# Key-value products in five sets of positions, and the first batch's loads and order of a float32 attention and expert kernel

## The chip, the cores and the metric

The kernel runs on one core of a Trainium2 chip. The metric is the time of one execution on the device in microseconds (us), as a median over runs. An engine of the core (TensorE or PE, VectorE or DVE, ScalarE or ACT, GpSimd or POOL, SyncE or SP) executes its own instructions in order; engines and transfers wait for each other through semaphores. "PEld" in a profile is TensorE's loading of stationary operands.

## The reference

All arrays are float32. Eight batches of eight heads with 576 positions of 64 numbers go through a linear attention with normalised rows, and the result, as 4608 tokens of 512, through four experts whose outputs are summed with normalised probabilities.

```python
kv = np.einsum('bhsd,bhse->bhde', k, v)          # q, k, v: (8, 8, 576, 64)
out = np.einsum('bhsd,bhde->bhse', q, kv)
rms = np.sqrt(np.mean(out * out, axis=-1, keepdims=True) + 1e-06)
x = (out / rms * g_norm)                          # to (4608, 512)
p = domain_probs / (domain_probs.sum(-1, keepdims=True) + 1e-09)
for e in range(4):                                # w1: (4, 512, 1024), w2: (4, 1024, 512)
    h = np.maximum(x @ w1[e], 0.0)
    out += p[:, e:e + 1] * (h @ w2[e])
```

## The kernel before

**Tiles and stages.** The tokens are nine chunks of 512: chunk b holds the first 512 positions of batch b, and the ninth holds the last 64 positions of all eight batches. A stage s is one expert with one chunk, 36 stages in all; TensorE's row of stages is the long part of the kernel. Attention of batch 0 stands at the very start, that of batch c + 1 is woven into stage c of the first expert. The matrix products of the experts use schemes with seven products in place of eight, at two levels (`up`, line 914 in the profile, for x by w1; `down`, line 1128, and `down_deep`, line 1203, for h by w2), so that sums of blocks of weights, of x and of h must be formed beforehand: `combine` (line 362) on DVE or POOL. The first stage's x by w1 is a plain product, `up_plain` (line 1001).

**Attention of a batch** works on four pairs of heads. A pair's q (128 partitions by four positions by two heads), k and v are loaded by SP (`load`, line 368). q is turned by four transpositions on TensorE (line 653) and copied by ACT (line 658). The key-value product (line 667, `key_values`) puts 96 partitions of k and v side by side, each with six positions (KP = 96, KR = 6): for each of the six it adds one product per head, 64 columns by 64, into one bank, the two heads in different halves of its partitions. ACT copies the sums (line 680); `attend` (line 693) multiplies q by them; `scaled` squares (ACT, line 566), sums (DVE, line 573), takes the power -1/2 (POOL, lines 580 and 584) and multiplies (DVE, line 593); the result is turned again (line 711) and copied with the gain by ACT (line 719). Batch 0 handles one pair at a time, the others two (`groups`). The last 64 positions of a batch go the same way in one piece: lines 737, 755, 771.

**Hardware passes.** A float32 product is executed as two passes and a transposition as one; the profile counts passes.

**Order.** No engine's order is written by hand. Each operation is added to a `Plan` with a key (its place in the stages) and a cost that the author gives; `layout` runs a small model of the engines and takes the operations in the order of keys and due times. It also gives out the buffers: `kv` has four slots, `big` 29, `small` eight, and the banks of PSUM are pairs `u1`, `u2`, `db`, `ab`. SP's loads are taken in strict order of keys, and at most eight transfers are in flight (`LANES`); the ninth waits for the landing of the first. Where the plan sees TensorE without data ahead of the first stage, it lays fillers (`idle`, line 1355): two transpositions of the identity into a free bank.

Keys that matter here: `attention(0, -2.0, 1.3, 0.1)`, `weights_1(0, -2.5, 0.02, 0.3)` (loads of the first expert's w1 and the place of its sums), `x_forms(0, 0.3)` (sums of x), `weights_2(0, 0.25, 0.02, 7.6)`, and in `up_plain`

```python
op = plan.add(
    key + span * i / 8 - (1.1 if i < 2 and dh == 0 else 0.0), pe(2, NT), product,
```

Of the kernel before, what the change touches and what calls it, by code (L numbers as in the profile page):

```python
# [232 lines left out]
def kernel(  # L233
# [36 lines left out]
    nc = tc.nc  # L270
# [4 lines left out]
    NT = 512  # L275
# [3 lines left out]
    NCH = B + 1  # L279
    HN = NT // 2  # L280
    HF = F // 2
    KR = 6
    KP = S // KR
    EPS = 1e-6
    NBLK = NCH * NR
    assert H * D == DM == NT and D == 64 and P == 128 and NPAIR == 4 and F == 1024
    assert REM == D and REM * B == NT and KP * KR == S and KP <= P

    const = ctx.enter_context(tc.tile_pool(name="const", bufs=1))
    pool = ctx.enter_context(tc.tile_pool(name="pool", bufs=1))  # L290
# [75 lines left out]
    def load(key, buf, dst, src, kb, reads=(), also=()):  # L366
        plan.add(
            key, SPC, lambda eng: nc.sync.dma_start(out=dst(), in_=src), reads=reads,  # L368
            parts=[buf] + list(also), kb=kb,
        )  # L370
# [232 lines left out]
    def attention(b, key, span, rem):  # L603
# [6 lines left out]
        at = lambda j: key + span * j / (NPAIR + 1)  # L610
        qTs, kvs = {}, {}

        def load_pair(hp):
            hs = slice(2 * hp, 2 * hp + 2)
            n = f"{b}_{hp}"
            kind = "kv" if b or hp < 2 else "big"
            kt, vt, qt = Buf(kind, f"k{n}"), Buf(kind, f"v{n}"), Buf("small", f"q{n}")
            want = at(hp) - 0.25 if b else key - 1 + 0.1 * hp
            for r in range(2):
                load(  # L620
                    want, qt,
                    lambda qt=qt, r=r: qt.ap[:].rearrange(
                        "p (r h d) -> p r h d", h=2, d=D)[:, :, r, :],
                    q[b, 2 * hp + r, 0:NT, :].rearrange("(p r) d -> p r d", r=NR), 128 if b else 157,
                )
            for t, src in ((kt, k), (vt, v)):
                load(
                    want, t,
                    lambda t=t: t.ap[0:KP, 0:2 * KR * D].rearrange("p (h x) -> p h x", h=2),
                    src[b, hs].rearrange("h (p j) d -> p h (j d)", j=KR), 288 if b else 241,  # L630
                )
            return kt, vt, qt

        def kv_rows(t):
            return t.ap[0:KP, 0:2 * KR * D].rearrange("p (h j d) -> p h j d", h=2, d=D)

        groups = ((0,), (1,), (2,), (3,)) if b == 0 else ((0, 1), (2, 3))
        for g, pairs in enumerate(groups):
# [4 lines left out]
            for o, hp in enumerate(pairs):  # L643
                kvs[hp] = kv, o
                kt, vt, qt = load_pair(hp)
                held.append((kt, vt))
                bank = Buf("ab", f"qT{b}_{hp}")
                qT = qTs[hp] = Buf("small", f"qT{b}_{hp}")

                def turn(eng, bank=bank, qt=qt):  # L650
                    for r in range(NR):
                        rs = slice(r * P, (r + 1) * P)
                        nc.tensor.transpose(bank.ap[:, rs], qt.ap[:, rs], ident[:])  # L653

                plan.add(at(hp), pe(4, P, 1), turn, reads=[qt], writes=[bank])
                plan.add(
                    at(hp), act(NT),
                    lambda eng, bank=bank, qT=qT: nc.scalar.activation(
                        out=qT.ap[:], in_=bank.ap[:], func=ACT.Copy),
                    reads=[bank], writes=[qT],  # L660
                )

            def key_values(eng, bank=kbank, held=held):
                for o, (kt, vt) in enumerate(held):
                    for j in range(KR):
                        for r in range(2):
                            nc.tensor.matmul(  # L667
                                bank.ap[r * D:(r + 1) * D, o * D:(o + 1) * D],
                                lhsT=kv_rows(kt)[:, r, j, :], rhs=kv_rows(vt)[:, r, j, :],
                                start=(j == 0), stop=(j == KR - 1), skip_group_check=True,  # L670
                            )

            size = len(pairs)
            plan.add(
                at(pairs[-1]), {"PE": 0.73 * size + 0.2}, key_values,
                reads=[t for ts in held for t in ts], writes=[kbank],
            )
            plan.add(
# [2 lines left out]
                    out=to.ap[:, 0:size * D], in_=bank.ap[:, 0:size * D], func=ACT.Copy),  # L681
                reads=[kbank], writes=[kv],
            )
            raw = [Buf(("db", "u2")[r] if b == 0 else "ab" if b > 1 else "db", f"raw{n}_{r}") for r in range(2)]

            def attend(eng, raw=raw, kv=kv, pairs=pairs):
                for o, hp in enumerate(pairs):
# [300 lines left out]
    def up_plain(s, e, c, key, span):  # L988
# [4 lines left out]
        for i in range(8):  # L993
            uh, a, u = i // 4, i // 2 % 2, i % 2
            bank = Buf("u1" if a == 0 else "u2", f"up{s}_{i}")
            for dh in range(2):
                w, low = corners[uh, dh]

                def product(eng, w=w, bank=bank, dh=dh, ut=2 * a + u):
# [5 lines left out]
                        )  # L1005

                op = plan.add(
                    key + span * i / 8 - (1.1 if i < 2 and dh == 0 else 0.0), pe(2, NT), product,
                    reads=[w, low, xh[dh]], **({"parts": [bank]} if dh else {"writes": [bank]}),
                )  # L1010
                op.marks = bank, NT
# [297 lines left out]

    plan.add(-2.85, {"SP": 1.1}, load_gains, writes=[gains], kb=1)  # L1310
    attention(0, -2.0, 1.3, 0.1)
    sums_1 = weights_1(0, -2.5, 0.02, 0.3)
    up_plain(0, 0, 0, 0.0, 1.0)
    sums_1()
    x_forms(0, 0.3)
    x_views = {}
    inner = {0: weights_2(0, 0.25, 0.02, 7.6)}
    norm_probs(0.3)
    for e in range(E):
        for c in range(NCH):  # L1320
            s = e * NCH + c
            if e == 0 and c + 1 < B:
                attention(c + 1, s - 0.1, 0.8, s + 0.5)
            if e + 1 < E and c == NCH - 1:
                weights_1(e + 1, s + 0.0, 0.12, s + 0.4)()
                inner[e + 1] = weights_2(e + 1, s + 1.0, 0.13, s + 1.55)
            if s + 1 < E * NCH:
                if e == 0 and c + 1 < NCH:
                    x_views[s + 1] = x_forms(c + 1, s + 0.7)
# [76 lines left out]
```

## Time and profile before

| What | Value |
|---|---|
| median of 7 runs | 1717.48 us (1717.08 to 1717.93) |
| profiled execution, its own time | 1717.84 us |
| its span, first to last instruction | 1716.0 us |
| TensorE's granted clock | 0.999 of full speed |
| TensorE's passes | 15564 |
| DVE, ACT, POOL busy | 72%, 57%, 40% of the span |
| DMA, 24 to 66 us | 95% of 16 engines, 262 GB/s |
| DMA, 420 us to the end | 50% of 16 engines, 123 GB/s |

A row of a timeline gives the start and the length in us of a run of like instructions, then engine, line, operation, the tiles written and read, the shape, and the number of passes. Lengths overlap by the latency of a pass, since passes are pipelined: what a run costs is the distance from its start to the start of the next row. A row of the waits gives the engine and line that waited, who ended the wait, the total, the count and the longest.

### The profile page before, as it was taken

The numbers are of one execution on the slowest core, as the hardware profiler recorded it, in microseconds if no ns is written. First come the engines' busy times: TensorE is split into PE (matmuls) and PEld (weight loads), VectorE is DVE, ScalarE is ACT, GpSimd is POOL, SyncE is SP. The second block draws the span as 40 slices with busy tenths as digits, with TensorE's granted clock in tenths as the row PEclk, the third lists the DMA queues.
The fourth block names the chain that finished last, engine by engine and source line by source line (L and its number), as shares of the span: only waits on it lengthen the run. The fifth ranks groups of instructions, "written<-read, shape, count | busy, mean of one in ns | idle before, by whom it ended". The sixth has DMA issues, their size and how long they took to land.

```text
span 1716.0 us, 39187 instructions
## 1 busy us (share of the span) xinstructions
PE 1709.1 (100%) x15564; PEld 1651.3 (96%) x15564; DVE 1239.2 (72%) x1992; ACT 973.5 (57%) x2378; POOL 692.4 (40%) x655
## 2 busy tenths in 40 slices
PE   9999999999999999999999999999999999999998
PEld 7799999999999999999999999999999999999998
DVE  4855565466678887777788787777788787777774
ACT  3455454455446556565666566656666666666562
POOL 3533332233433432333355554433355544433331
PEclk9999999999999999999999999999999999999999
DMA  9854543543365445353568444444478444444442
GB/s 234 277 165 145 182 145 123 149 142 142 130 160 148 107 109 113 97 116 102 140 178 178 114 106 111 111 112 112 112 182 200 111 112 111 112 111 111 102 108 49
DMA packets 156567, 230.42 MB, mean 134 GB/s; under 512 B 49888, under 2 KB 97248, under 8 KB 156384
## 3 DMA queue, kind: packets, MB, share of 16 engines
q1 hardware_dynamic: 133312, 191.21, 36.4%
q0 software_dynamic: 23072, 36.71, 14.2%
q8 instruction: 122, 2.00, 0.5%
q14 instruction: 61, 0.50, 0.1%
HBM read 154.74 MB, written 73.14 MB: 133 GB/s over the span
## 4 chain that ended last, share of the span: by engine, by line
PE 99%; DMA 1%; SPq 0%; issue 0%; DVE 0%
PE u L914 45%; PE db L1203 21%; PE ab L1203 13%; PE db L1128 12%; PE u L1001 2%; PE ab L667 1%; PE ab L711 1%; PE ab L693 1%; PE ab L653 1%; PE u L1128 1%; DMA big<-in_v_dram 0%; PE ab L1128 0%; DMA kv<-in_v_dram 0%; SPq L368 0%; PE ab L755 0%; PE ab L771 0%
## 5 line engine op out<-in xcount | busy, mean ns | idle before, releaser
L362 DVE TENSOR_TENSOR big<-big,big 128x1024 f32<-128x1024 f32 (+1 forms) x435 | 437.9, 1019 | 16.7 <-ACT big L897 6.6
L914 PE MATMUL u<-xf,big 128*128 128x128 f32 x2816 | 412.5, 275 | 0.0
L914 PE MATMUL u<-xf,w1y 128*128 128x128 f32 x2652 | 391.2, 275 | 0.0
L914 PEld LDWEIGHTS u<-xf,big 128*128 128x128 f32 x2816 | 364.3, 192 | 2.0
L941 DVE TENSOR_TENSOR big<-u,snap 128x256 f32<-128x256 f32 x436 | 183.7, 421 | 239.7 <-PE u L914 155.5
L914 PEld LDWEIGHTS u<-xf,w1y 128*128 128x128 f32 x2652 | 343.7, 192 | 1.7
L933 ACT ACTIVATE snap<-u 128x256 f32<-128x256 f32 x490 | 187.5, 383 | 185.3 <-PE u L914 152.3
L362 POOL TENSOR_TENSOR big<-big,big 128x256 f32<-128x256 f32 (+1 forms) x138 | 183.4, 1344 | 164.3 <-DVE big L362 45.0
L933 ACT ACTIVATE big<-u 128x256 f32<-128x256 f32 x436 | 166.4, 383 | 99.1 <-PE u L914 73.5
L1128 PE MATMUL db<-big,big 128*128 128x256 f32 x920 | 217.0, 380 | 0.0
L1128 PEld LDWEIGHTS db<-big,big 128*128 128x128 f32 x920 | 166.8, 190 | 18.6
L1203 PE MATMUL db<-big,big 128*128 128x128 f32 x1304 | 178.1, 275 | 0.0
L1203 PEld LDWEIGHTS db<-big,big 128*128 128x128 f32 x1304 | 161.7, 192 | 0.1
L897 ACT ACTIVATE big<-big 128x1024 f32<-128x1024 f32 x126 | 132.4, 1051 | 4.5 <-DVE big L362 3.1
L1231 ACT ACTIVATE snap<-db 128x256 f32<-128x256 f32 x216 | 76.8, 356 | 102.1 <-PE db L1203 98.6
L362 POOL TENSOR_TENSOR big<-big 128x512 f32<-128x512 f32 (+1 forms) x67 | 82.2, 1229 | 119.3 <-DVE big L362 60.0
L1098 POOL DMA_DIRECT2D out_dram<-big x100 | 90.6, 1031 | 56.2 <-ACT big L1075 37.0
L1269 POOL TENSOR_TENSOR big<-big 128x512 f32<-128x512 f32 x26 | 33.0, 1269 | 198.3 <-DVE big L362 168.5
L914 PE MATMUL u<-xf,small 128*128 128x128 f32 x720 | 108.4, 275 | 0.0
L933 ACT ACTIVATE u<-u 128x256 f32<-128x256 f32 x245 | 90.9, 371 | 29.4 <-PE u L914 13.2
L1203 PE MATMUL ab<-kv,big 128*128 128x128 f32 x740 | 106.0, 275 | 0.0
L1203 PE MATMUL db<-kv,big 128*128 128x128 f32 x720 | 103.3, 275 | 0.0
(211 smaller groups left out, 2872.8 us busy)
## 6 DMA issues: line engine op xcount, KB each, us to landing
xf<-x SPq DMA_DIRECT2D x108, 512.0 KB, 3.7
out_dram<-big POOLq DMA_DIRECT2D x84, 256.0 KB, 5.8
xf<-x_h SPq DMA_DIRECT2D x81, 256.0 KB, 3.1
xf<-x SPq DMA_DIRECT2D x81, 256.0 KB, 3.3
x<-xf SPq DMA_DIRECT2D x36, 512.0 KB, 3.7
big<-in_moe_w_dram SPq DMA_DIRECT2D x31, 512.0 KB, 5.7
small<-in_q_dram SPq DMA_DIRECT2D x72, 128.0 KB, 4.2
kv<-in_k_dram SPq DMA_DIRECT2D x30, 288.0 KB, 4.5
```

Source lines behind the costliest of these rows:

```text
L362: lambda eng: adder(eng).tensor_tensor(out=out_(), in0=a(), in1=b(), op=op),
L653: nc.tensor.transpose(bank.ap[:, rs], qt.ap[:, rs], ident[:])
L897: lambda eng: nc.scalar.activation(out=b.ap[:], in_=b.ap[:], func=ACT.Relu),
L914: nc.tensor.matmul(ps.ap[:, u * P:(u + 1) * P], lhsT=w1f[e][m][mm][1]()[:, u * P:(u + 1) * P], rhs=views[m][mm][1](), start=(mm in (1, 5) ...
L933: lambda eng: nc.scalar.activation(out=where(), in_=ps.ap[:, 0:HN], func=ACT.Copy),
L941: lambda eng: nc.vector.tensor_tensor(out=block(whole, a, t), in0=src.ap[:, 0:HN], in1=add_.ap[:], op=ALU.add),
L1001: nc.tensor.matmul(bank.ap[:], lhsT=two(w.ap[:])[:, kt, ut * P:(ut + 1) * P], rhs=two(xh[dh].ap[:])[:, kt, :], start=(dh == kt == 0), stop ...
L1098: nc.gpsimd.dma_start(out=dst, in_=cell(i)[parts, :], accum_op=ALU.add)
L1128: nc.tensor.matmul(ps.ap[:, 0:HN], lhsT=four(h[m])[:, kt // 2, t, kt % 2, :], rhs=w2f[e][m].ap[:, kt * HN:(kt + 1) * HN], start=(m in (1, ...
L1203: nc.tensor.matmul(ps.ap[:, o * P:(o + 1) * P], lhsT=b.ap[:, col:col + P], rhs=w2q[e][m][mm][1]()[:, kt, :], start=(mm in (1, 5) and o == ...
L1231: lambda eng: nc.scalar.activation(out=where(), in_=group_of(ps.ap), func=ACT.Copy),
L1269: lambda eng: adder(eng).tensor_tensor(out=whole(to), in0=whole(a), in1=whole(b), op=ALU.add),
```

## The change

- **Key-value products.** In batches 1 to 7, k and v are laid in two parts: 120 partitions with four positions each (480 positions), and 96 partitions with one (the last 96). `key_values` then has five sets in place of six, four with 120 rows and one with 96. Each of k and v is loaded in two transfers, with pieces of 1024 and 256 bytes in place of 1536. Batch 0 keeps six positions on 96 partitions. The planner's cost of the product for these batches is 0.61 per pair in place of 0.73.
- **First batch's q.** One load per pair in place of two, in pieces of 1024 bytes (four positions of one head) in place of 256. The heads now lie one after the other, and the turn is eight products with the identity, 64 columns of stationary operand each, in place of four transpositions.
- **First batch's banks.** The two raw results of a pair are in `db`, `u2`, `u1`, `db` for pairs 0 to 3, in place of one in `db` and one in `u2` for every pair.
- **`up_plain`.** The first-half products of i = 0 to 3 (not 0 and 1) get an early key, in the order 2, 3, 0, 1.
- **Keys.** Small shifts for the sums of w1, of x and of w2, for batch 1, and for later experts' weights. Through the planner they move instructions on all engines.

In the program of instructions TensorE has 56 key-value products fewer (384 to 328), 54 fillers for 92, and for batch 0 32 products in place of 16 transpositions. SP issues 56 loads of k and v more and four of q fewer. DVE has 32 instructions more, POOL 32 fewer.

```diff
+        splits = ((120, 4, 0), (96, 1, 480)) if b else ((96, 6, 0),)
...
-            for r in range(2):
+            if b == 0:
                 load(
-                    want, qt,
-                    lambda qt=qt, r=r: qt.ap[:].rearrange(
-                        "p (r h d) -> p r h d", h=2, d=D)[:, :, r, :],
-                    q[b, 2 * hp + r, 0:NT, :].rearrange("(p r) d -> p r d", r=NR), 128 if b else 157,
-                )
+                    want, qt, lambda qt=qt: qt.ap[:].rearrange("p (h x) -> p h x", h=2),
+                    q[b, hs, 0:NT, :].rearrange("h (p r) d -> p h (r d)", r=NR), 172,
+                )
...
             for t, src in ((kt, k), (vt, v)):
-                load(
-                    want, t,
-                    lambda t=t: t.ap[0:KP, 0:2 * KR * D].rearrange("p (h x) -> p h x", h=2),
-                    src[b, hs].rearrange("h (p j) d -> p h (j d)", j=KR), 288 if b else 241,
-                )
+                at_ = 0
+                for rows, n_, size in splits:
+                    kb = rows * n_ // 2
+                    load(
+                        want, t,
+                        lambda t=t, at_=at_, rows=rows, n_=n_: t.ap[0:rows, at_:at_ + 2 * n_ * D]
+                        .rearrange("p (h x) -> p h x", h=2),
+                        src[b, hs, size:size + rows * n_].rearrange("h (p j) d -> p h (j d)", j=n_),
+                        kb if b else 241,
+                    )
+                    at_ += 2 * n_ * D
...
-                        nc.tensor.transpose(bank.ap[:, rs], qt.ap[:, rs], ident[:])
+                        if b:
+                            nc.tensor.transpose(bank.ap[:, rs], qt.ap[:, rs], ident[:])
+                            continue
+                        for o in range(2):
+                            at = (o * NR + r) * D
+                            nc.tensor.matmul(
+                                bank.ap[o * D:(o + 1) * D, rs], lhsT=qt.ap[:, at:at + D],
+                                rhs=ident[:],
+                            )
...
-                    for j in range(KR):
+                    sets = list(zip(kv_rows(kt), kv_rows(vt)))
+                    for j, (ks, vs) in enumerate(sets):
                         for r in range(2):
                             nc.tensor.matmul(
                                 bank.ap[r * D:(r + 1) * D, o * D:(o + 1) * D],
-                                lhsT=kv_rows(kt)[:, r, j, :], rhs=kv_rows(vt)[:, r, j, :],
-                                start=(j == 0), stop=(j == KR - 1), skip_group_check=True,
+                                lhsT=ks[r], rhs=vs[r], start=(j == 0),
+                                stop=(j == len(sets) - 1), skip_group_check=True,
                             )
...
-            raw = [Buf(("db", "u2")[r] if b == 0 else "ab" if b > 1 else "db", f"raw{n}_{r}") for r in range(2)]
+            kind = ("db", "u2", "u1", "db")[g] if b == 0 else "ab" if b > 1 else "db"
+            raw = [Buf(kind, f"raw{n}_{r}") for r in range(2)]
...
-                    key + span * i / 8 - (1.1 if i < 2 and dh == 0 else 0.0), pe(2, NT), product,
+                    key - 0.89 + 0.01 * (i ^ 2) if i < 4 and dh == 0 else key + span * i / 8,
+                    pe(2, NT), product,
...
-    sums_1 = weights_1(0, -2.5, 0.02, 0.3)
-    up_plain(0, 0, 0, 0.0, 1.0)
+    sums_1 = weights_1(0, -2.50, 0.02, 0.26)
+    up_plain(0, 0, 0, 0.0, 1.00)
     sums_1()
-    x_forms(0, 0.3)
+    x_forms(0, 0.45)
     x_views = {}
-    inner = {0: weights_2(0, 0.25, 0.02, 7.6)}
-    norm_probs(0.3)
+    inner = {0: weights_2(0, 0.25, 0.04, 7.60)}
+    norm_probs(0.30)
...
-                attention(c + 1, s - 0.1, 0.8, s + 0.5)
+                attention(c + 1, s - 0.1 + 0.03 * (s == 0), 0.8, s + 0.5)
...
-                weights_1(e + 1, s + 0.0, 0.12, s + 0.4)()
-                inner[e + 1] = weights_2(e + 1, s + 1.0, 0.13, s + 1.55)
+                weights_1(e + 1, s + 0.0, 0.12, s + 0.47)()
+                inner[e + 1] = weights_2(e + 1, s + 1.00, 0.13, s + 1.54)
```

## The prediction

> **What bounds the kernel now.** I read the busy shares, then the chain of waits, then TensorE's waits, then the timeline of the first 66 us. The page says TensorE works all the time:
>
> ```profile
> PE 1709.1 (100%) x15564; PEld 1651.3 (96%) x15564; DVE 1239.2 (72%) x1992; ACT 973.5 (57%) x2378; POOL 692.4 (40%) x655
> PE 99%; DMA 1%; SPq 0%; issue 0%; DVE 0%
> ```
>
> The other engines have room, and the chain is TensorE except for 1%. TensorE's list of waits has two entries:
>
> ```profile
> PE ab L1355 <- POOL ident masks.py:199: 1.4, 1, 1.4
> PE ab L667 <- DMA big<-in_v_dram: 1.0, 1, 1.0
> ```
>
> So the time is the sum of TensorE's instructions plus 2.4 us. But "busy" includes fillers (L1355), products of the identity that the planner lays where it expects TensorE to lack data. The start in TensorE's timeline (start, length; x counts hardware passes, two for each float32 product, one for a transposition):
>
> ```profile
> 1.35 4.96 PE L1355 MATMUL ab<-ident 128*128 128x128 f32 x22 [1.35 <-POOL ident masks.py:199]
> 6.10 0.98 PE L653 MATMUL ab<-ident,small 128*128 128x128 f32 x4
> ...
> 18.79 0.82 PE L1355 MATMUL ab<-ident 128*128 128x128 f32 x6
> 20.58 0.92 PE L667 MATMUL ab<-big,big 96*64 96x64 f32 x24 [0.97 <-DMA big<-in_v_dram]
> ...
> 23.79 3.60 PE L1001 MATMUL u<-big,big 128*128 128x512 f32 x8
> 27.22 0.60 PE L711 MATMUL ab<-ident,big 128*128 128x128 f32 x4
> 27.66 1.26 PE L1355 MATMUL ab<-ident 128*128 128x128 f32 x10
> 28.75 0.60 PE L711 MATMUL ab<-ident,big 128*128 128x128 f32 x4
> ...
> 33.65 0.60 PE L653 MATMUL ab<-ident,small 128*128 128x128 f32 x4
> 34.18 0.68 PE L755 MATMUL db<-kvbd,small 64*64 64x64 f32 x16
> 34.79 1.62 PE L667 MATMUL ab<-kv,kv 96*64 96x64 f32 x48
> 36.34 1.98 PE L1001 MATMUL u<-big,big 128*128 128x512 f32 x4
> ```
>
> Dense work begins at 23.79; before it fillers stand in for data. The last v of the first batch lands at 20.44 (7.87 us after its issue, in the chain):
>
> ```profile
> 12.57 7.87 DMA big<-in_v_dram
> ```
>
> Outside the span of 1716.0 lie 1.84 us of the profiled execution's 1717.84; that execution is 0.36 above the median of 1717.48. I sum against 1717.84 and take off 0.36. Measurement tells about 0.2% (3.4 us) from no change.
>
> **1. Five sets for six, batches 1 to 7.** A set is two heads by two passes. The L667 group of 24 passes runs from 12.06 to the next row at 12.91 (0.85), that of 48 from 34.79 to 36.34 (1.55): 24 passes are six sets in 0.70, so a set is 0.117 us. 28 pairs drop one: **-3.28 us**. Passes follow 64 columns, and the timeline cannot show a 120-row pass. Bounds: dearer by 25% for 25% more rows would give +0.8 instead; the 64-, 96- and 128-row rows of equal width show no such growth (64-row and 96-row passes last 221 to 224 ns alike), so I take -3.28.
> One rule speaks against this edit. Going from 128*128 to a narrower form and back costs extra: L653's four passes take 0.44 before a wide product (28.75 to 29.19 for L711's like), 0.53 before a narrow one (33.65 to 34.18); the first narrow pass pair is 0.05 late, the way back 0.10: about 0.12 a change. The Trainium skill, "TensorEngine Tiling (Array Packing)", Key Properties, says that changing the tiling mode drains TensorE. The new groups mix 120 and 96 rows, three row changes in each of 14 groups. If those are mode changes they cost 42 x 0.15 = 6.3 us. The page's list of modes has only 128, 64 and 32 rows, so 96 and 120 would be one mode and cost 0. No row here has 120 rows; I take 0 and keep 6.3.
>
> **2. Loads of k and v in two parts.** 56 loads more, on SP's queue. Each part is a wait of L667, and behind it on TensorE stands everything. From the third batch on, v lands 9.7 to 29 us ahead of L667 (landing 63.34, use 73.02, is the tightest), while SP issues take 0.45 to 0.62: four more for two pairs, about 2 us, are hidden. In batch 1 the slacks are 0.94 (landing 33.85, use 34.79) and 3.55 (48.15, 51.70): counted in 5. The remainder has 256-byte pieces; "DMA: Bandwidth & Descriptors", Specifications, wants 512 bytes or more for full rate. By the packet records of this trace 256-byte pieces take 18 to 21 ns and 1536-byte ones 91 to 94, 13 and 16 bytes per ns: nearly the same. By the row a remainder of 12 pieces per engine is 0.24 us and the four-set part (16 pieces of 1024, 46 to 56 ns) 0.8 to 0.9, in all like the 1.1 of now[...].
>
> **3. The start.** q of batch 0 comes in one load of 1024-byte pieces per pair: SP issues four loads fewer (0.55 to 0.63 each) and 256 KB take 0.75 to 0.97 us instead of about 1.1. Its turn becomes eight products of 64 columns, 16 passes. No row shows them; nearest is L667, where two column halves overlap (a pair of passes in 58 ns at 64 columns), so 111 ns per pair at 128 columns: 0.89 per turn for 0.44. Bounds: 0.44, and 1.74 if halves do not overlap (+3.4 in all, partly in place of the wait for v).
> The instruction order of the new kernel gives TensorE's row to the first L1001; with fillers at 0.216 until about 6.5 us (22 in 4.75) and 0.109 after: 18 fillers to 5.24; turn (half pace) 6.9; 10 fillers 8.1; keys-values 0.75 to 8.85; turn 0.89 to 9.74; attention (32 passes) 0.68 to 10.42; 4 fillers 10.95; keys-values 11.70; turn 12.59; attention 13.27; 6 fillers 14.02; keys-values 14.77; turn 15.66; attention 16.34; 2 fillers and L711's kind 17.09; fourth keys-values 17.94; 8 fillers, L711's kind, attention, 6 fillers 20.6. That is **-3.2** if data are there.
> Are they? v of pair 3 must land by 17.1 instead of 20.44. The first load's second half alone saves about 1 to 1.5 us before bandwidth binds (q lands at 3.45 and 5.48 now), each later pair 0.12 to 0.35: landing 17.5 to 19.0. Taken 18.0: a wait of **+0.9** (bounds 0.4 and 3.4, the last if v lands as now). What comes after it in order, L711's kind and L1001, is late with it; the first w1 load lands 1.1 after v and is not later.
>
> **4. Sums and products reordered.** Up products i = 2, 3, 0, 1 start before the halves of x are complete, so the ten fillers at 27.66 go: **-1.09**. The chain of pair 3 (squares, sum, power on POOL 1.9, two products) ends 4.3 us after its attention now (23.1 to 27.4); the new order leaves 0.66 + 3.44 + 0.44 + 1.72 = 6.3 before its L711: no wait.
> From the first L1001 on the new order changes form 93 times, the old 102: 9 x 0.12 = **-1.1**. DVE and POOL exchange sums (31 more small ones on DVE); DVE is idle 28% of the span and POOL 60%, which covers it; without cover the 31 would cost 0.28 each.
>
> **5. New waits in the stretch to 66 us**, where everything is some 3 us early. The transposition of batch 1's remainder (L771 now) follows two L711 groups directly and needs a bank that ScalarE must first copy out: 0.2 + 0.69 + 0.1 after the first group against 0.44 of the second: **+0.5** (0 to 1.1). Batch 1's first keys-values come at 21.5 + 3.44 + 0.44 + 1.72 + 0.44 + 1.72 + 0.53 + 0.39 + 1.72 + 0.53 = 32.4. Its v lands at 33.85 now; 2.4 earlier, as pair 3's does, and up to four issues of 0.5 later gives 31.5 to 33.5: **+0.5** (0 to 1.5). The second L1128 needs h6: relu, POOL 2.35, DVE 1.2, now 5.9 us after the last L1001 (64.9 to 70.76, slack 0.26); new order 0.97 + 0.5 + 0.39 + 1.73 + 0.88 + 0.45 = 4.9, POOL free a little earlier: **+0.5** (0 to 1.5). Behind them on TensorE waits all that follows.
>
> Sum: -3.28 - 3.2 + 0.9 - 1.09 - 1.1 + 0.5 + 0.5 + 0.5 = -6.3. 1717.84 - 6.3 = 1711.5; median **1711.2**.
>
> **Rivals.**
> A, no new wait: without the 2.4 us, 1708.8. Against: 20.58 already waits for v. 0.12.
> B, the start is bound by v as now, q's pieces hide nothing: L667 at 20.5, then 0.85 + 0.87 + 0.53 + 0.63 + 0.66: L1001 at 24.0, +0.25 for -2.3; TensorE no longer early, other waits 1.0 for 1.5: -6.3 + 2.55 - 0.5 = -4.2, time 1713.3. For: 7.87 from issue to landing shows a deep queue. 0.20.
> C, row changes drain: 1711.2 + 6.3 = 1717.5, the change does nothing one can measure. For: each change of form in the rows costs 0.12 or so. Against: the page's modes. 0.12.
> D, slower: SP's queue. Between 17.10 and 42.18 SP issues without rest, and issues of k and v there last 0.45 to 1.80. Eight more fall before batch 1's two groups. Each costing t delays the second group by 8t, less its 3.55 slack and the 2.4 that data come earlier, plus the 3.2 that TensorE comes earlier: wait 8t - 2.75. At 1.8 that is 11.65, in place of 0.5: 1722.4. It decides from the t that eats the gain and 3.4 more: 8t - 2.75 = 0.5 + 6.3 + 3.4, t = 1.6. Against: the usual issue is 0.5, and the same bytes move. 0.06.
>
> **How the numbers follow.** The main case has 0.50: 1711.2, its own range 1709 to 1714. Its gain passes 3.4 us, as do A's and B's: faster 0.82. C is the no-change case: 0.12. D: 0.06. The range leaves out D and most of C and takes the bounds in: 1708.4 to 1716.5.
>
> **What would show it.** L667 groups of 40 passes in 1.32 us between starts, without a step at the 96-row set (C: 1.7 or more). First L1001 at 21 to 22 (B: 24). L667's wait for v near 1 us; new waits at L771's and L1128's kind below 1.5 each. After 66 us no wait. It is wrong if L667 groups keep 1.55, if waits of several us stand before 66 us, or if experts' rows wait at all.

## The result and the profile after

The changed kernel takes 1713.24 us (median of 15 runs, 1711.52 to 1715.05), the kernel before beside it 1717.24 (35 runs, 1716.47 to 1720.36): a ratio of 0.9975 (95% interval 0.9968 to 0.9982), a gain of 4.0 us for 6.3 foretold. The profiled execution has a span of 1711.3 us and a time of its own of 1713.09; that of before had 1716.0 and 1717.84.

The page of the changed kernel: busy shares, the queue that brings instructions (packets, MB, share of the DMA engines), and the chain of waits.

```profile
PE 1701.6 (99%) x15462; PEld 1644.0 (96%) x15462; DVE 1229.6 (72%) x2024; ACT 971.6 (57%) x2378; POOL 693.9 (41%) x623
...
q8 instruction: 122, 2.00, 0.5%
...
PE 97%; POOL 1%; DVE 1%; DMA 1%; issue 0%; ACT 0%; POOLq 0%; DVEq 0%; ACTq 0%
```

TensorE is busy 7.5 us less and the span is only 4.7 us shorter: waits have come. TensorE's list of waits has six entries now, for two before:

```profile
PE ab L697 <- issue: 1.7, 1, 1.7
PE ab L1387 <- POOL ident masks.py:199: 1.4, 1, 1.4
PE u L945 <- ACT snap L964: 0.9, 1, 0.9
PE db L1160 <- DVE big L591: 0.5, 1, 0.5
PE ab L802 <- ACT big L750: 0.5, 1, 0.5
PE ab L1387 <- issue: 0.4, 1, 0.4
```

Lines have moved: L697 is the key-value product (L667 before), L678 the first batch's turn of q, L724 the attention, L742 and L802 the turns of its result, L1032 `up_plain`, L945 `up`, L1160 `down`, L1387 the fillers. The wait for v, which the prediction kept at 0.9 us, is not in the list. In its place stand two rows whose releaser is "issue": TensorE waited for nothing that the profile shows. TensorE's timeline shows where:

```profile
10.58 0.92 PE L697 MATMUL ab<-kv,kv 96*64 96x64 f32 x24
...
13.74 0.91 PE L697 MATMUL ab<-big,big 96*64 96x64 f32 x23
16.33 0.22 PE L697 MATMUL ab<-big,big 96*64 96x64 f32 x1 [1.68 <-issue]
...
18.79 0.92 PE L697 MATMUL ab<-big,big 96*64 96x64 f32 x24
...
22.76 0.38 PE L1387 MATMUL ab<-ident 128*128 128x128 f32 x2 [0.38 <-issue]
22.98 1.88 PE L1032 MATMUL u<-big,big 128*128 128x512 f32 x4
```

A group of 24 passes on operands that are all there breaks off after 23; the last pass comes 1.9 us later. No operand can be late for one pass of a group. The same happens inside fillers at 22.1, for 0.65 us from start to start. Without the two stops (1.88 and 0.49 beyond the usual distance) the first L1032 would have come at 20.6, where the prediction's walk through the order put it with data there; it came at 22.98, for 23.79 before.

Four more places of the same timeline, the turns behind the first L1032, the five sets of batch 1, the stretch at 62 us and a wait at 908 us:

```profile
26.41 0.60 PE L742 MATMUL ab<-ident,big 128*128 128x128 f32 x4
26.85 1.88 PE L1032 MATMUL u<-big,big 128*128 128x512 f32 x4
28.57 0.60 PE L742 MATMUL ab<-ident,big 128*128 128x128 f32 x4
...
34.00 1.39 PE L697 MATMUL ab<-kv,kv 120*64 120x64 f32 x40
35.31 0.68 PE L786 MATMUL db<-kvbd,small 64*64 64x64 f32 x16
...
61.07 1.04 PE L742 MATMUL ab<-ident,big 128*128 128x128 f32 x8
62.56 0.46 PE L802 MATMUL ab<-ident,small 64*128 64x64 f32 x4 [0.45 <-ACT big L750]
63.57 1.99 PE L1160 MATMUL db<-big,big 128*128 128x256 f32 x8 [0.55 <-DVE big L591]
...
907.46 1.06 PE L1235 MATMUL ab<-big,big 128*128 128x128 f32 x8
909.47 0.71 PE L945 MATMUL u<-xf,small 128*128 128x128 f32 x4 [0.95 <-ACT snap L964]
```

From 34.00 to 35.31 are 1.31 us for 40 passes, 1.55 for 48 before. The ten fillers between the turns behind L1032 are gone. The waits of 0.45 and 0.55 cost 0.62 each from start to start (1.49 us for eight passes that elsewhere take 0.87, and 1.01 for four that take 0.39), that at 908 us 1.1.

### The profile page after: what moved, and what is told of

Read it like the earlier page. It is cut to its first block, busy times and chain, and to the rows that moved or that the text cites. A ratio compares the mean times of both kernels' runs of the same rounds, so it can differ in the third digit from the quotient of the medians.

```text
span 1711.3 us, 39139 instructions
## 1 busy us (share of the span) xinstructions
PE 1701.6 (99%) x15462; PEld 1644.0 (96%) x15462; DVE 1229.6 (72%) x2024; ACT 971.6 (57%) x2378; POOL 693.9 (41%) x623
## 4 chain that ended last, share of the span: by engine, by line
PE 97%; POOL 1%; DVE 1%; DMA 1%; issue 0%; ACT 0%; POOLq 0%; DVEq 0%; ACTq 0%
PE u L945 45%; PE db L1235 21%; PE ab L1235 13%; PE db L1160 12%; PE ab L697 1%; PE ab L742 1%; PE ab L724 1%; PE ab L674 1%; PE u L1160 1%; POOL rt L582 1%; DMA out_dram<-big 1%; PE u L1032 1%; PE ab L1387 0%; PE ab L1160 0%; DVE big L360 0%; POOL big L360 0%
## 5 line engine op out<-in xcount | busy, mean ns | idle before, releaser
L360 DVE TENSOR_TENSOR big<-big,big 128x1024 f32<-128x1024 f32 (+1 forms) x467 | 452.5, 986 | 38.1 <-ACT big L928 19.9
L945 PE MATMUL u<-xf,big 128*128 128x128 f32 x2960 | 431.2, 275 | 0.0
L945 PE MATMUL u<-xf,w1y 128*128 128x128 f32 x2652 | 391.2, 276 | 0.0
L945 PEld LDWEIGHTS u<-xf,big 128*128 128x128 f32 x2960 | 381.3, 192 | 1.6
L945 PEld LDWEIGHTS u<-xf,w1y 128*128 128x128 f32 x2652 | 343.3, 192 | 1.7
L360 POOL TENSOR_TENSOR big<-big,big 128x256 f32<-128x256 f32 (+1 forms) x153 | 201.8, 1326 | 123.7 <-DVE big L360 56.6
L1160 PE MATMUL db<-big,big 128*128 128x256 f32 x920 | 217.7, 380 | 0.5 <-DVE big L591 0.5
L1160 PEld LDWEIGHTS db<-big,big 128*128 128x128 f32 x920 | 166.2, 190 | 18.6 <-DVE big L591 0.7
L1235 PE MATMUL db<-big,big 128*128 128x128 f32 x1232 | 167.0, 275 | 0.0
L1235 PEld LDWEIGHTS db<-big,big 128*128 128x128 f32 x1232 | 152.1, 192 | 0.1
L1235 PE MATMUL db<-kv,big 128*128 128x128 f32 x808 | 115.4, 275 | 0.0
L1235 PE MATMUL ab<-kv,big 128*128 128x128 f32 x788 | 112.8, 275 | 0.0
L964 ACT ACTIVATE u<-u 128x256 f32<-128x256 f32 x245 | 90.8, 371 | 30.6 <-PE u L945 10.6
L1235 PEld LDWEIGHTS db<-kv,big 128*128 128x128 f32 x808 | 102.6, 192 | 0.0
L1301 POOL TENSOR_TENSOR big<-big 128x512 f32<-128x512 f32 x22 | 27.9, 1270 | 180.4 <-DVE big L360 178.0
```

Source lines behind the costliest of these rows:

```text
L360: lambda eng: adder(eng).tensor_tensor(out=out_(), in0=a(), in1=b(), op=op),
L945: nc.tensor.matmul(ps.ap[:, u * P:(u + 1) * P], lhsT=w1f[e][m][mm][1]()[:, u * P:(u + 1) * P], rhs=views[m][mm][1](), start=(mm in (1, 5) ...
L964: lambda eng: nc.scalar.activation(out=where(), in_=ps.ap[:, 0:HN], func=ACT.Copy),
L1160: nc.tensor.matmul(ps.ap[:, 0:HN], lhsT=four(h[m])[:, kt // 2, t, kt % 2, :], rhs=w2f[e][m].ap[:, kt * HN:(kt + 1) * HN], start=(m in (1, ...
L1235: nc.tensor.matmul(ps.ap[:, o * P:(o + 1) * P], lhsT=b.ap[:, col:col + P], rhs=w2q[e][m][mm][1]()[:, kt, :], start=(mm in (1, 5) and o == ...
L1301: lambda eng: adder(eng).tensor_tensor(out=whole(to), in0=whole(a), in1=whole(b), op=ALU.add),
```

## The experiments

**Two theories for the stops.** TensorE's instructions are themselves transfers: the page counts 122 packets on the instruction queue, 2.00 MB, so 16 KB each, and the 31,390 TensorE records (weight loads and passes) of the kernel before by its 122 packets are 257. *Theory of blocks*: TensorE gets its instructions in blocks of 256, only the next block is fetched ahead, and where 256 instructions pass quicker than a fetch comes, TensorE runs dry. The first stop begins at record 448, the second at record 704, 256 later. *Rival*: a wait of this order of work that the records don't show, tied to the place. What follows tells them apart, and sizes the parts of the change.

**The five sets alone.** The kernel before with k and v in two parts and five sets in batches 1 to 7; order and all else as before.

```diff
...
+        splits = ((120, 4, 0), (96, 1, 480)) if b else ((96, 6, 0),)
...
-                    for j in range(KR):
+                    sets = list(zip(kv_rows(kt), kv_rows(vt)))
+                    for j, (ks, vs) in enumerate(sets):
...
```

> The kernel before with part 1 alone: batches 1 to 7 in five sets of 120 and 96 rows, each k and v in two transfers, every engine's order as before (L667 has 20 products for 24). If a set costs 0.117 us and the row change nothing: 28 sets, -3.3 us, L667 groups of 40 passes 1.31 us apart from the next row, start unchanged at 23.8. If 120 to 96 rows drains TensorE (0.15 a change, 42 changes): +3.0 us, groups of about 1.76. If the loads in two parts hold TensorE up: a new wait of L667 on k or v in batch 1, near 34 or 51 us.

Measured: 1713.76 us (11 runs) beside 1717.08 for before, ratio 0.998 (0.9972 to 0.9989): -3.3 us. Its timeline:

```profile
22.54 3.60 PE L1018 MATMUL u<-big,big 128*128 128x512 f32 x8
...
33.54 1.39 PE L684 MATMUL ab<-kv,kv 120*64 120x64 f32 x40
34.85 1.98 PE L1018 MATMUL u<-big,big 128*128 128x512 f32 x4
```

Again 1.31 from start to start, and no step between the sets of 120 and of 96 rows: from one set to the next pass 0.05 us, with the change of rows as without. There is no wait but that for the identity. The 28 transfers of k and 28 of v more cost nothing here. So most of the gain of the change is this one edit.

The start moved too, though the edit leaves it alone: this execution did not wait for v, and its first wide product came at 22.54, for 23.79 in the profile of before. The start thus differs by more than 1 us between executions of one order. What lies behind it does not: from the first wide product to the last pass are 1684.13 us here and 1687.29 in the kernel before, 3.16 less. That is the five sets without the luck of the start.

**The sets undone in the changed kernel**, batches 1 to 7 back at six sets of 96, one transfer each.

```diff
...
+                                out=t.ap[0:96, 0:12 * D].rearrange("p (h x) -> p h x", h=2),
+                                in_=src[b, hs].rearrange("h (p j) d -> p h (j d)", j=6),
...
-            for rows, n_, _ in splits:
+            for rows, n_ in ((96, 6),):
...
```

> The changed kernel with its first part alone undone: batches 1 to 7 take their key-value products again in six sets of 96 positions, with one transfer each for k and v; all orders, the first batch and everything else stay as changed. If the parts add (the five sets gave -3.3 us alone), this is 3.3 us longer than the changed kernel: 1716.5 us, ratio to the kernel before 0.9996. TensorE's stop of 1.5 to 2 us near 14.4 us stays, since nothing ahead of it is different; the groups of L697 last 1.57 again instead of 1.31. If instead the five sets are what makes something late behind 30 us, less than 3.3 comes back: 1714 to 1715.

Measured: 1716.02 us (11 runs), ratio 0.999 (0.9982 to 0.9999), against 0.9975 for the changed kernel. By the medians it gains 1.1 us on the kernel before and the changed kernel 4.0, so 2.9 us come back, within the uncertainty of the 3.3. All of the change but the sets is thus worth about 1.1 us (0.2 to 3.1); the prediction had 3.0 for it.

The stop at record 448 is there again, of 1.95 us, and behind it the granted clock fell to half (busy times by stretch: stretch, length, busy us of PE, PEld, DVE, ACT and POOL, granted clock, DMA share, GB/s), so that the turn of q lasted 1.98 us for 1.09 in the changed kernel, and the first L1034 came at 24.44:

```profile
16.90:20.20 3.30, 3.30 (x51) 2.85 (x51) 0.76 (x2) 1.03 (x3) 0.10 (x1) 0.51 1.04 364
```

```profile
16.91 1.98 PE L680 MATMUL ab<-ident,small 128*64 128x128 f32 x16
```

Where other executions of this kernel lose to the clock, that is in the 2.9 as well. Behind the start the trace is free of it: from the first wide product to the last pass it is 2.31 us longer than the changed kernel's, while the wait of 0.62 us at L1160 is gone and the waits near 908 and 1306 us are 0.35 less. Together these are 3.28 us.

**The stops put into the kernel before.** Eleven fillers there, from 10.6 us on, become four products of 64 columns in place of two transpositions: 132 records more in the same time, nothing else touched.

```diff
...
+        laid.append(bank)
+        if 21 <= len(laid) <= 31:
+            for j in range(4):
+                o = j % 2 * 64
+                nc.tensor.matmul(bank[o:o + 64, 0:64], lhsT=ident[:, o:o + 64], rhs=ident[:, 0:64],
+                                 start=True, stop=True, skip_group_check=True)
+            return
```

> The kernel before, with 11 fillers between 11 and 18 us laid as four products of 64 columns instead of two transpositions: the same TensorE time within 0.2 us, but 132 more instructions (12 each). The results are not touched. Theory I (TensorE's instructions come in blocks of 256, and it runs dry where a block has not come): a gap without a semaphore appears at about the 448th TensorE record, near 14.5 us, and ends some 1.4 us after the end of the first 16 KB instruction transfer, about 16.5 us; the wait for v at 19.3 shrinks by that, and the time rises by 0 to 1 us. Theory M (the gap belongs to the new kernel's q turn, its banks or its loads): no gap without a semaphore here, v is waited for as before, time within 0.3 us.

Measured: 1720.65 us (10 runs), ratio 1.0021 (1.0012 to 1.0031), +3.6 us. TensorE's waits and, below, its timeline:

```profile
PE ab L1360 <- issue: 1.3, 1, 1.3
PE ab L667 <- issue: 1.3, 1, 1.3
```

```profile
14.31 0.27 PE L1360 MATMUL ab<-ident 128*64 128x64 f32 x1
15.87 1.09 PE L1360 MATMUL ab<-ident 128*64 128x64 f32 x30 [1.29 <-issue]
```

Two stops without a semaphore, of 1.56 and 1.48 us, where none were, one between two products of the identity that need nothing. They begin at records 448 and 704. That is the theory of blocks; a wait tied to the changed kernel's order is ruled out. The price was larger than the 0 to 1 us expected, in part since the second block ran dry too. The profiled execution, the fastest of the ten, accounts for 1.5 us: its first L1001 comes at 25.27 for 23.79, and from there on it takes the same 1687.29 us as the kernel before. Where the median loses the other 2 us, no trace shows.

**Where the boundaries lie**, in six of the thirteen profiles. From the packet records of the instruction queue and the count of TensorE records (us from the span's start, one profiled execution each): when record 192 or 448 starts, when the next fetch begins and ends, when the last record before the boundary starts, and how long TensorE then stops.

```
                  record 192  fetch         record 447  stop | record 448  fetch         record 703  stop
before              10.71   14.00-15.12     17.67      none  |   17.68   20.70-21.80     27.99      none
changed              9.54   13.69-14.92     14.38      1.90  |   14.43   20.15-21.26     22.11      0.65
before, dense       10.29   13.17-14.39     14.31      1.56  |   14.31   20.21-21.27     21.17      1.48
q as before         10.06   13.21-14.46     17.02      none  |   17.03   20.33-21.44     28.15      none
early products       2.62    5.10-5.98      11.70      none  |   11.73   18.41-19.52     17.79      2.98
lean fillers         9.36   12.47-13.78     14.97      none  |   15.07   19.42-20.53     24.84      none
```

Over all thirteen profiles a fetch begins 2.5 to 4.2 us after record 192 and 2.6 to 6.7 us after record 448, and takes 0.9 to 1.4 us. Seven profiles stop at record 448 and six at record 704, for 0.5 to 3.0 us from start to start, and in all thirteen stops the first new record starts 1.30 to 1.50 us after the end of the fetch. In the changed kernel 4.15 + 1.23 + 1.41 = 6.8 us, while its records 192 to 447 take 4.9 us: a stop of 1.9. In the kernel before they took 7.0, and its block was usable 5.8 us after record 192. Later in the kernel 256 records of L945 (128 passes of 112 ns) take 14 us, and no stop shows.

Why the first fetches begin so late is open. In these stretches the sixteen DMA engines are full (a share of 1.04 to 1.11 between record and fetch in the changed kernel); from 420 us on in the kernel before, with a share of 0.50, a fetch typically begins at its record, within 4 us to either side. That fits a fetch that waits behind other transfers, but no run separates it.

**Earlier boundaries.** In the changed kernel the first six fillers become eight products of 32 columns, 168 records more ahead of record 192.

```diff
...
+        laid.append(bank)
+        if 1 <= len(laid) <= 6:
+            for j in range(8):
+                o = j % 4 * 32
+                nc.tensor.matmul(bank[o:o + 32, 0:32], lhsT=ident[:, o:o + 32], rhs=ident[:, 0:32],
+                                 start=True, stop=True, skip_group_check=True)
+            return
```

> The changed kernel, with its first six fillers laid as eight products of 32 columns each: 168 more instructions before the first q has landed, all engines' order else the same. Theory I: the first block of 256 is used up some 5 us earlier, its successor asked for earlier, and the boundaries fall 168 records earlier in the work: the gap of 1.9 us in the third key-value product goes or shrinks below 0.5, the next boundary (about 17 us) waits up to 1.3; first L1032 at 21.5 to 22.5 instead of 23.0 and the time 0.5 to 1.5 us below the changed kernel's 1713.2. Theory M: the gap stays in the third key-value product at 14.4 us, and the time does not move.

Measured: 1717.52 us (11 runs, 1712.87 to 1720.36), ratio 1.0 (0.9991 to 1.0009): 4 us worse than the changed kernel, a miss. Its timeline, and its busy times by stretch (stretch, length, busy us of PE, PEld, DVE, ACT and POOL, granted clock, DMA share, GB/s):

```profile
17.38 0.67 PE L724 MATMUL u<-kvbd,small 64*64 64x64 f32 x27
20.82 0.33 PE L724 MATMUL u<-kvbd,small 64*64 64x64 f32 x5 [2.77 <-issue]
...
21.95 1.55 PE L697 MATMUL ab<-big,big 96*64 96x64 f32 x24
```

```profile
16.00:17.90 1.90, 1.61 (x46) 1.37 (x44) 0.51 (x3) 0.62 (x2) 1.67 (x2) 1.00 1.07 230
18.00:20.70 2.70, 0.06 (x2) 0.00 (x0) 0.55 (x2) 0.10 (x1) 0.00 (x0) 1.00 1.04 366
21.00:23.40 2.40, 2.40 (x35) 2.02 (x32) 0.69 (x1) 1.35 (x3) 0.66 (x2) 0.66 1.12 343
23.40:26.00 2.60, 2.60 (x30) 2.41 (x32) 0.00 (x0) 0.39 (x2) 1.17 (x1) 0.66 1.15 200
```

The stop at record 448 is gone, as it should be, but record 704 now falls into the attention at 17.8, with its fetch only at 18.41: a stop of 3 us. Behind it the granted clock is 0.66 on average over two stretches (by the clock records, half for 3.41 us from 21.77 on), and 24 passes of L697 last 1.55 for 0.92. The first L1032 comes at 27.06, 4.1 us later than in the changed kernel, which is nearly all of the loss. The expectation had up to 1.3 us for this boundary; with the fetch 6.7 us behind record 448 it was 3.

**The later experts' weight keys as before**, all else changed, for the wait at 908 us.

```diff
-                weights_1(e + 1, s + 0.0, 0.12, s + 0.47)()
-                inner[e + 1] = weights_2(e + 1, s + 1.00, 0.13, s + 1.54)
+                weights_1(e + 1, s + 0.0, 0.12, s + 0.4)()
+                inner[e + 1] = weights_2(e + 1, s + 1.0, 0.13, s + 1.55)
```

> The changed kernel with the two keys of the later experts' weights as before (0.4 and 1.55); the order is the same to some 120 us. If the 1.1 us wait of L945 for ScalarE at 908 us comes of these keys, it goes and the time falls by 1.1 us to about 1712.1. If it is chance of one execution or of another edit, a wait of that kind stays and the time is within 0.5 of 1713.2. In any case no change at the start.

Measured: 1711.17 us (5 runs), ratio 0.9968 (0.9955 to 0.998). TensorE's waits:

```profile
PE ab L1387 <- POOL ident masks.py:199: 1.4, 1, 1.4
PE ab L1387 <- issue: 0.6, 1, 0.6
PE db L1160 <- DVE big L591: 0.5, 1, 0.5
PE ab L697 <- DMA kv<-in_v_dram: 0.5, 2, 0.3
PE ab L802 <- ACT big L750: 0.5, 1, 0.5
```

The row of L945 is gone, so these keys made that wait. The time against the changed kernel's is 1.2 to 2 us less, but the intervals of the two overlap. The traces are sharper. From 800 us to the last pass this one and the five others that have these keys as before (the kernel before among them) agree to 0.01 us; the seven with the new keys take 1.2 to 1.9 us more, the changed kernel 1.58 (1.2 of it at 908 us, the rest near 1306 and 1334). In this execution record 448 came 1.25 us after the end of its fetch, and no stop stands there; the fetch began at 12.61, for 13.69 in the changed kernel, with the same order up to there. The 0.6 in the list is the stop at record 704.

**The first batch's q as before**, two loads in 256-byte pieces and four transpositions per pair; sets, banks, sums and keys as changed. TensorE's order up to the first L1032 is then the one before the change.

```diff
...
-                    q[b, hs, 0:NT, :].rearrange("h (p r) d -> p h (r d)", r=NR), 172,
...
+                        q[b, 2 * hp + r, 0:NT, :].rearrange("(p r) d -> p r d", r=NR), 157,
...
-                        if b:
+                        if True:
...
```

> The changed kernel with q of the first batch loaded and turned as before the change (two loads in 256-byte pieces, four transpositions per pair). TensorE's order up to the first product of L1001's kind is then the one before the change, fillers and all, and so are SP's loads; five sets and the sums behind it stay as changed. As the prediction sized the start, it gives -2.3 us, and this kernel takes 1713.2 + 2.3 = 1715.5 us. As the traces size it, the start gave only 0.8 (first L1001 at 22.98 for 23.79, with 2.4 us of stops at records 448 and 704), and this kernel takes 1714.0: 96 records fewer, no stop at 448 or 704, first product of L1001's kind at 23.8. If the two waits of 0.6 us near 62 us come from TensorE being early, they shrink as well: 1713.0 to 1713.5.

Measured: 1713.42 us (10 runs), ratio 0.9975 (0.9966 to 0.9984). The changed kernel unaltered, on the same chip:

> The changed kernel unaltered, beside the next two on one chip. By the theory of blocks its time varies with the moment at which the second half of its first 1000 TensorE records is fetched: 1711.5 to 1715 as before, median 1713.2, and in the profile a stop without a semaphore of 0 to 2 us at record 448 and of 0 to 0.8 at record 704, each ending 1.4 to 1.5 us after the fetch before it.

Measured: 1712.58 us (6 runs, 1711.53 to 1713.05), ratio 0.997 (0.9958 to 0.9982), with stops of 1.1 and 0.4 us in the list of waits. So by the medians q's part of the new start is worth 0.2 to 0.8 us, and the intervals can't tell it from nothing. At 2.3 us the kernel with the old q would have taken 1715.5; its slowest run took 1713.90. The timeline with the old q:

```profile
19.78 0.92 PE L700 MATMUL ab<-big,big 96*64 96x64 f32 x24 [0.83 <-DMA big<-in_v_dram]
...
22.99 1.88 PE L1035 MATMUL u<-big,big 128*128 128x512 f32 x4
```

It waits 0.83 us for v, has no stop at a boundary, and reaches the first `up_plain` at 22.99; the changed kernel does at 22.98. What the new start takes off TensorE's wait for v and its fillers it gives back at the boundaries of its instructions. These two moments are single executions: the old q came to the first wide product at 22.54 (five sets alone), 22.99 and 23.79 (before), the new one, with the fillers unaltered, at 22.16 (old late keys), 22.71 (twice), 22.98 and, where the clock fell, 24.44.

**Two pairs in flight for three**: the first batch's raw results in `db` and `u2` for every pair.

```diff
-            kind = ("db", "u2", "u1", "db")[g] if b == 0 else "ab" if b > 1 else "db"
-            raw = [Buf(kind, f"raw{n}_{r}") for r in range(2)]
+            raw = [Buf(("db", "u2")[r] if b == 0 else "ab" if b > 1 else "db", f"raw{n}_{r}") for r in range(2)]
```

> The changed kernel with the raw results of the first batch in the banks of before the change (db and u2 for every pair), so that two pairs are in flight, not three; q as changed. Fillers ahead of the first L1032: 54 as in the changed kernel, but the last two before it are moved ahead of the fourth key-values. By the theory of blocks the 192 records ahead are the same and the stop at 448 is the same 1.5 to 2 us. If the third pair in flight was worth something, the first L1032 comes later than 22.98, by up to 0.7 (an attention that follows its products of key-values by less); else 1713.2 us as the changed kernel.

Measured: 1713.08 us (9 runs), ratio 0.9975 (0.9965 to 0.9985), first product at 22.7, the stop at 448 in place. The third pair is worth nothing that can be measured.

**Fewer filler instructions.** Pairs of fillers after 10 us become one product of the identity with 256 or 512 columns, of nearly the same duration (the first such pair takes 0.63 us between starts, for 0.58); then the same with the old late keys; then all fillers so.

```diff
...
+            nc.tensor.matmul(
+                bank[:, 0:blocks * P].rearrange("p (a t) -> p a t", t=P), lhsT=ident[:],
+                rhs=ident[:].unsqueeze(1).to_broadcast([P, blocks, P]),
+                start=True, stop=True, skip_group_check=True)
...
```

> The changed kernel with the fillers after 10 us in fewer instructions: pairs of them become one product of the identity with 256 or 512 columns, which lasts as long but is 4 or 12 TensorE records fewer. 8 records fewer lie ahead of record 448, some 24 ahead of record 704. If the stops near 14.4 and 22.1 us come from TensorE's instructions arriving in blocks of 256 records, record 448 is reached about 0.2 us later and its stop is 0 to 0.3 us shorter; record 704 moves from the last fillers into the products of L1032, some 2 us later, and the second stop is gone: 0.5 to 0.8 us less than the changed kernel, 1712.5 us. If the stops come from something else (a wait that the profile doesn't show, at these places in the order), they stay at 14.4 and 22.1 and the time is the changed kernel's, 1713.2.

> The same fewer filler instructions after 10 us, and the later experts' weight keys as before the change (which took the wait of 1.1 us at 908 us away). By the theory of blocks the two add: 1711.2 - 0.6 = 1710.6 us; by the other 1711.2.

> As the one before, with all runs of fillers in wide products, those from 1.3 us on too: 36 records fewer ahead of record 192, 44 ahead of 448, some 60 ahead of 704. By the theory of blocks record 448 is reached 0.7 to 1.2 us later than in the changed kernel. If the fetch of the next block waits for TensorE to have come to a certain record (192), it starts as much later and the stop keeps its length of up to 1.9 us; if it waits for the DMA queues, which are full up to 20 us, it starts at 12.5 to 14 as it did and the stop shrinks to 0 to 1 us. Time 1710.0 us by the second, 1710.6 by the first.

Measured: 1713.28 us (8 runs, 1711.18 to 1713.99), ratio 0.9975 (0.9965 to 0.9986); 1711.61 (5 runs), 0.9965 (0.9952 to 0.9977); 1711.75 (5 runs), 0.9965 (0.9952 to 0.9977). In all three profiles record 704 has moved into L742 or the turns behind the first L1032 and its stop is gone, as expected. The times missed: the medians show none of the 0.6 us, the first of them lies at the 1713.2 of the other theory, and the others lie above both of their values. The first of them was profiled in its fastest execution, and its timeline has no stop at 448 either:

```profile
14.21 0.92 PE L697 MATMUL ab<-big,big 96*64 96x64 f32 x24
14.96 1.25 PE L678 MATMUL ab<-ident,small 128*64 128x128 f32 x16
...
17.57 0.92 PE L697 MATMUL ab<-big,big 96*64 96x64 f32 x24
...
21.29 3.60 PE L1032 MATMUL u<-big,big 128*128 128x512 f32 x8
```

The key-values pass without a break, v is not waited for, and the first L1032 comes at 21.29, 2.5 us ahead of the kernel before. This execution took 1711.18 us. The start's forecast of -2.3 is thus what the order can give when the instructions are there; in both profiles of the changed kernel they weren't. With all fillers thinned out, record 192 came at 10.11 and its fetch began at 14.35, with 9.29 and 13.10 in the kernel ahead of it in this list, and stops of 0.87 and 0.76 stay. That the fetch moves with the record, and not with the queues alone, is plainer in the run with earlier boundaries (2.62 and 5.10). Fewer records ahead of the start of a fetch were not seen to help.

The versions with the old late keys are the shortest, 1711.2 to 1711.8 us: faster than the kernel before by 0.32 to 0.35%, and not told apart from the changed kernel by their intervals.

## Why the prediction was right, and where it was not

The forecast of faster was right, and 1713.24 lies in the range, 2.0 above the value. By its steps:

- **Five sets: right.** -3.28 foretold, -3.3 measured alone, -3.16 in the trace behind the start. The rival of row changes that drain is out: 40 passes take 1.31 us, no step at the 96-row set. The Trainium skill, "TensorEngine Tiling (Array Packing)", Available Configurations, lists row modes of 128, 64 and 32 rows alone; that 96 and 120 rows count as one agrees with these groups, and the 6.3 us did not come. One support of the step was thinner than it reads: the 221 to 224 ns are lengths of single passes that overlap, and no row of before has 128 rows at 64 columns.
- **Loads in two parts: right.** No wait for k or v of the later batches in the changed kernel; in batch 1 v landed at 31.41 and was used at 34.00, so the +0.5 was not paid. The rival of SP's queue (+3.4 and more from 1.6 us an issue) did not happen.
- **The start: mis-sized, and the step that failed.** Foretold -3.2 + 0.9 = -2.3. The walk ends right to 0.1 us with the two stops taken out, with some luck: it had the first key-values at 8.1 for 7.65, and the rows behind took a little more than it gave them, which made that up. v landed at 17.29 for 18.0 foretold. But the sum asked of each instruction only whether its data are there, and not whether the instruction is. The edit turns 8 records per q into 32, and 192 to 447 pass in 4.9 us for 7.0. The stops cost 1.88 + 0.49 = 2.37 in the profiled execution, in place of the wait of 0.9; first L1032 at 22.98 is -0.8. With the old q in the changed kernel the time is the same within 0.8 us, and the start of one order differs by 0.8 us and more between executions, so that even the 0.8 is not shown.
- **Ten fillers: right**, gone at -1.09.
- **Changes of form: not shown.** From the first L1032 to the last pass the trace is 3.65 us shorter. Of it -3.16 are the sets, -1.09 the fillers, +0.62, +0.62 and +1.58 the waits; what is left is -2.2, for -1.1 foretold. No run separates it.
- **New waits: one of three.** The 0.62 at L802 is the bank that ScalarE must copy (0.5 foretold). The second L1160 did not wait for h6. The first did, 0.62, for a bank that DVE empties (`scaled`, L591), which was not in the sum. With six sets, in an execution that comes there 1.9 us later (1.5 of it from the start, where the clock fell), this wait is gone and that at L802 is still there. With the old q, whose order differs there, both are gone and one of 0.58 for ScalarE stands at 63.4 in their place: they belong to the order, and not to an early start alone.
- **"Wrong if experts' rows wait at all": they did**, for 1.58 us in all, most of it at 908 us. The later experts' keys, for which the prediction has no term, made it.

The sum as it should have stood in the profiled execution: -3.16 - 0.8 - 1.09 - 2.2 + 0.62 + 0.62 + 1.58 = -4.4; the last pass starts 4.46 us earlier. It closes because the 2.2 is what is left over. That the forecast came within 2 us owes something to this: the start gave 1.5 us less than foretold and the waits behind it took 1.3 more, while the unexplained rest gave 1.1 more. Rival B had the size (1713.3) for another cause: it held v's landing to be the bound, and v came 3 us earlier. Rival A, no new wait, is out by the list of waits.

## What to carry to other kernels

Count an engine's instructions, not only their time, where many short ones stand in a stretch that is full of transfers: here a block of 256 TensorE records was usable 5 to 9 us after the boundary before it (delay, fetch and some 1.4 us, worked out from the thirteen profiles), and 256 records that passed quicker ran dry. A wait whose releaser is "issue", inside a group whose operands are all there, is the mark of it; then look at where the next boundary falls too before moving the first. And a key shifted by 0.07 far behind the change belongs in the sum like the rest. Compare traces behind the last place that varies, too: there six of them agree to 0.01 us, where medians of ten runs could not tell 1 us.

## What the runs showed of the hardware

- TensorE stops without a semaphore at records 448 and 704, 256 apart, until 1.3 to 1.5 us after the end of a 16 KB packet on the instruction queue. The Trainium skill, "Runtime: NRT & Kernel Launch", Instruction fetch mechanics, describes refills in blocks of 256 instructions and calls the cost of a boundary mostly hidden; the blocks agree with these traces, and the cost here was 0 to 3 us a boundary in the first 25 us. The page gives TensorE room for 2048 instructions; in the runs it ran dry at 448 and 704 with a single block on its way, so no more than one block ahead was there, and the measurement decides.
- The first two fetches start 2.5 to 6.7 us after the boundary before them, while the DMA engines are full or nearly so (a share of 0.93 to 1.11 in the changed kernel and in the run with earlier boundaries); with the same order up to there, the first began at 12.61 in one execution and at 13.69 in another. The spread of the times does not show this: 3.5 us for the changed kernel, 3.9 for the kernel before, whose profile has no stop.
- After a stop of 2.98 us (earlier boundaries) and after one of 1.95 us (sets undone) the granted clock fell to half for 3.41 us; after one of 1.90 us (changed kernel) it did not. The clock records last multiples of 3.41 us (3.41, 10.24, 17.07). In the 3.41 us ahead of the two falls TensorE had no pass for 2.46 and 1.56 us; cut the same way, no other such stretch from the first clock record to 25 us, in any profile, has more than 1.29. So where a stop falls in these stretches may decide, and not its length alone; no run tests it.
